# The w_gate products of six wide tiles as seven block products, in pairs with those of w_val

## The chip, the core and the metric

The kernel runs on one core of a Trainium2 chip. A core has five engines that work side by side, each through its own instructions in order: TensorE (PE in the profile; its weight loads are PEld), VectorE (DVE), ScalarE (ACT), GpSimd (POOL) and SyncE (SP). They wait for each other on semaphores. PE writes its products to PSUM, here eight banks of 128 x 512 fp32; all other data lies in SBUF. The metric is the device time of one execution in microseconds (us); lower is better. All times below are us unless another unit stands beside them.

## The reference

Sliding-window causal attention (8 batches, 8 heads, 576 positions of 64 values, window 64) is followed by a gated feed-forward layer on the 4608 rows of 512 values that it gives:

```python
scores = scale * np.matmul(q, k.transpose(0, 1, 3, 2))
mask = (rel >= 0) & (rel < 64)              # rel = pos[:, None] - pos[None, :]
attn = softmax(np.where(mask, scores, -1e9))
x = np.matmul(attn, v)                      # as 4608 x 512
gate = np.maximum(x @ w_gate, 0.0)          # 512 x 1536
val = x @ w_val                             # 512 x 1536
return (gate * val @ w_out)                 # 1536 x 512
```

## The kernel before

The 4608 rows are taken in ten tiles: tiles 0 to 3 of 384 rows (narrow), tiles 4 to 9 of 512 rows (wide). For each tile there is a hidden stage (x times w_gate and w_val, relu, product: g_sb) and an output stage (g_sb times w_out, to PSUM, by ACT to SBUF, by an SP transfer to memory). The attention of the coming tiles is woven in between: loads of q, k and v are issued on POOL's queue (L173, L199), POOL or DVE spreads v (L208, L210), DVE transposes q and k (L193), PE makes scores (L253), ACT takes exp (L287, L389), DVE masks (L292, L394), PE multiplies by v (L311, L422), DVE normalises and transposes into xt, the tile's x (channels on the partitions, four chunks of 128).

The order of all engines is written by hand. A planner, `Weaver` (W), holds a clock in us that follows PE's work and a heap of callbacks with due times; `W.at(t, fn)` plans one, `W.advance` issues those that are due before PE's next product is issued, `W.pop` issues the next one early. What is issued goes at once into its engine's queue, so due times set the order in the queues, not the times on the chip.

In the narrow tiles (`hidden`) four relus of w_gate's products go by ACT to a tile `r4` (two buffers), then w_val's four products are multiplied with them by DVE.

In the wide tiles (`fast_hidden`) w_val's product is made by a scheme of Strassen's kind (Winograd's form): a product of 2 x 2 blocks takes seven block products, P1 to P7, in place of eight. The blocks halve the channels (k), the columns of w_val (HF = 6 chunks of 128 apart) and the 512 rows of the tile (HT = 256). It needs four sums of blocks of w_val, `vs`, formed once by POOL (`w_form`, L480, planned during tile 2), and four of x per tile, `xc`, formed by DVE (`x_form`, L459). A tile's hidden stage is three groups j of 4 chunks each. One block product is four matmuls of 256 columns (L573); one w_gate product is four matmuls of 512 columns (L582), with four such in a group and a relu for each (L586). The order of a group on PE is

```python
P1, gate(2), P6, P2, gate(3), P5, P7, gate(0), P4, gate(1), P3
```

P1, P6, P7 and P4 are added up in one bank A, of which ACT takes a copy (`snap`, L593) after P1, after P6 and after P7; P2 goes to bank B, P5 and P3 to bank C. DVE adds a copy to B or C (`vsum`, L600): P1's copy with P2, P7's copy with P5 and P6's copy with P5 + P3 are three of the four quarters of val, and what stands in A after P4 is the fourth, which DVE multiplies with its relu straight from the bank (L613). The other three products relu x val are POOL's (L606). `bank()` hands out PSUM banks in the order in which they became free.

The output stage of a wide tile (`fast_output`) goes over four blocks of 128 rows (L658, 12 matmuls each); the first two need the products of the first 256 rows, the last two those of the second half. Ahead of the blocks come the next tile's products with v (two halves) and the scores of the tile after it (two quads). k and q loads are planned by `plan_batch`, 12 us of the planner's clock ahead of a given time (`qk_ahead`).

Of the kernel before, what the change touches and what calls it, by code (L numbers as in the profile page):

```python
# [15 lines left out]
SUB = mybir.AluOpType.subtract  # L16
ONE_ONE = struct.unpack("<f", struct.pack("<I", 0x3C003C00))[0]


# [27 lines left out]
def kernel(  # L47
# [10 lines left out]
    nc = tc.nc  # L58
# [34 lines left out]
    wo = persist.tile([128, NF, DM], FP16)  # L93
    HF = NF // 2
    vs = persist.tile([128, 4, 2, 128 * HF], FP16)
    qTs = [persist.tile([128, 2, S, 2], FP16, name=f"qT{i}") for i in range(2)]
    kTs = [persist.tile([128, 2, 64 + S, 2], FP16, name=f"kT{i}") for i in range(2)]

# [265 lines left out]
    def bank():  # L364

        while not free:
            W.pop()
        return free.pop(0)
# [83 lines left out]
    def x_form(t, n):  # L452

        if t not in xcs:
            xcs[t] = x_sb.tile([128, 4, 2, HT], FP16, name="xc", tag="xt")
        xt, xc = xt_tile(t), xcs[t]
        b11, b12, b21, b22 = (xt[:, 2 * k:2 * k + 2, HT * h:HT * h + HT] for k in range(2) for h in range(2))
        x, y = ((b12, b11), (b22, xc[:, 0]), (b22, b12), (b21, xc[:, 1]))[n]
        nc.vector.tensor_tensor(xc[:, n], x, y, SUB)  # L459
        if n == 3:  # L460
            normed[0] = t

    def values(t, hh, T, banks=None):

        t_pv(t, hh, banks or [bank() for _ in range(3)], banks is None)
        W.clock += 0.62
        W.at(T + 0.7, lambda: t_recip(t, hh))
        for i, k in enumerate((2, 0, 1)):
            W.at(T + 1.2 + 0.5 * i, lambda k=k: t_norm(t, hh, k))
        W.at(T + 2.7, lambda: t_turn(t, hh))  # L470
        for n in ((0,), (1, 2, 3))[hh]:
            W.at(T + 4.0 + 0.4 * n, lambda n=n: x_form(t, n))

    def w_form(n, j):

        c = slice(256 * j, 256 * j + 256)
        f = slice(256 * j + 128 * HF, 256 * j + 128 * HF + 256)
        a11, a12, a21, a22 = wv[:, 0:2, c], wv[:, 2:4, c], wv[:, 0:2, f], wv[:, 2:4, f]
        x, y, op = ((a21, a22, ADD), (vs[:, 0, :, c], a11, SUB), (a11, a21, SUB), (a12, vs[:, 1, :, c], SUB))[n]
        nc.gpsimd.tensor_tensor(vs[:, n, :, c], x, y, op)  # L480

    def plan_batch(b, load, trans):
        for i, (name, hh) in enumerate((n, hh) for n in "kq" for hh in range(2)):
# [23 lines left out]
    def hidden(t, spans, f0=0, f1=NF, each=1):  # L507
# [18 lines left out]
            done.update(dict.fromkeys(range(f, f + w), c0 + n))  # L526

        for fb in range(f0, f1, each):
            r4 = f_sb.tile([128, 4, WT], FP32, name="r4", bufs=2)
            r_sbs = {}  # L530
            for i, wt in enumerate((wg, wv)):
                for c0, f in ((c0, f) for c0, _ in spans for f in range(fb, fb + each, w)):
# [6 lines left out]
                                             xt[:, c, c0:c0 + n], start=(c == 0), stop=(c == NC - 1))  # L539
                        W.clock += 4 * (n + 7) / 2400.0  # L540
                    if i == 0:
                        r_sb = r_sbs[c0, f] = r4[:, len(r_sbs)]
                        W.at(W.clock, lambda r_sb=r_sb, h=h: relu(r_sb, h))
                    else:
                        W.at(W.clock, lambda f=f, c0=c0, r_sb=r_sbs[c0, f], h=h: gate(f, c0, r_sb, h))

    def fast_hidden(t):

        g_sb, done = gs[t] = g_sb_p.tile([128, NF, WT], FP16, name="g_sb"), {}
        xt, xc = xt_tile(t), xcs[t]  # L550
        b11, b12, b21, b22 = (xt[:, 2 * k:2 * k + 2, HT * h:HT * h + HT] for k in range(2) for h in range(2))
        halves = lambda ap: ap.rearrange("p f (h n) -> p f h n", h=2)
        pair = lambda ap: ap.rearrange("p (f n) -> p f n", f=2)

        def group(j):
            c = slice(256 * j, 256 * j + 256)
            f = slice(256 * j + 128 * HF, 256 * j + 128 * HF + 256)
            r4 = f_sb.tile([128, 4, WT], FP32, name="r4", bufs=2)
            rh = halves(r4)
            gh = halves(g_sb)  # L560
            at = {}
            forms = {"P1": (wv[:, 0:2, c], b11), "P2": (wv[:, 2:4, c], b21), "P3": (vs[:, 3, :, c], b22),
                     "P4": (wv[:, 2:4, f], xc[:, 3]), "P5": (vs[:, 0, :, c], xc[:, 0]),
                     "P6": (vs[:, 1, :, c], xc[:, 1]), "P7": (vs[:, 2, :, c], xc[:, 2])}

            def product(name, to, first):
                W.advance(W.clock)
                if first:
                    at[to] = bank()
                w, x = forms[name]  # L570
                for i in range(2):
                    for k in range(2):
                        nc.tensor.matmul(at[to][:, HT * i:HT * i + HT], w[:, k, 128 * i:128 * i + 128], x[:, k],  # L573
                                         start=(first and i == 0 and k == 0), stop=(k == 1), skip_group_check=True)
                W.clock += 4 * (HT + 7) / 2400.0

            def gate(n):
                W.advance(W.clock)
                to = bank()
                ff = 2 * j + n % 2 + HF * (n // 2)  # L580
                for k in range(NC):
                    nc.tensor.matmul(to, wg[:, k, 128 * ff:128 * ff + 128], xt[:, k], start=(k == 0), stop=(k == NC - 1))  # L582
                W.clock += 4 * (WT + 7) / 2400.0

                def relu():
                    nc.scalar.activation(r4[:, n], to, ACT.Relu)  # L586
                    free.append(to)
                W.at(W.clock, relu)

            def snap(name):  # L590
                def copy():
                    at[name] = f_sb.tile([128, 512], FP32, name="snap", bufs=5)
                    nc.scalar.copy(at[name], at["A"])  # L593
                W.at(W.clock, copy)

            def add(delay, to, name, last, n, h):

                def summed():
                    v = f_sb.tile([128, 512], FP32, name="vsum", bufs=4)
                    nc.vector.tensor_tensor(v, at[to], at[name], ADD)  # L600
                    at["summed", n, h] = True
                    if last:
                        free.append(at[to])

                    def mult():
                        nc.gpsimd.tensor_tensor(gh[:, 2 * j + HF * n:2 * j + HF * n + 2, h], rh[:, 2 * n:2 * n + 2, h], pair(v), MUL)  # L606
                        done[2 * j + HF * n, h] = done[2 * j + HF * n + 1, h] = True
                    W.at(max(W.clock, at["relus", n]) + 0.7, mult)
                W.at(W.clock + delay, summed)

            def direct():
                def mult():
                    nc.vector.tensor_tensor(gh[:, 2 * j + HF:2 * j + HF + 2, 0], rh[:, 2:4, 0], pair(at["A"]), MUL)  # L613
                    free.append(at["A"])
                    done[2 * j + HF, 0] = done[2 * j + HF + 1, 0] = True
                W.at(W.clock + 0.2, mult)

            T = W.clock
            at["relus", 1], at["relus", 0] = T + 3.7, T + 6.8
            product("P1", "A", True)  # L620
            snap("a1")
            gate(2)
            product("P6", "A", False)
            snap("u2")
            product("P2", "B", True)
            add(0.1, "B", "a1", True, 0, 0)
            gate(3)
            product("P5", "C", True)
            product("P7", "A", False)
            snap("u3")  # L630
            add(0.8, "C", "u3", False, 1, 1)
            gate(0)
            product("P4", "A", False)
            direct()
            gate(1)
            while ("summed", 1, 1) not in at:
                W.pop()
            product("P3", "C", False)
            add(0.1, "C", "u2", True, 0, 1)

        for j in range(NF // 4):
            group(j)

    F_LAST = [f for j in range(NF // 4) for f in (2 * j + HF, 2 * j + HF + 1, 2 * j, 2 * j + 1)]

# [73 lines left out]
    with tc.manual_schedule():  # L719
# [132 lines left out]
        def ahead(t):  # L852
# [94 lines left out]
```

## Time and profile before

| | |
|---|---|
| median of 3 runs | 322.11 |
| lowest, highest run | 321.64, 323.05 |
| the profiled execution: span, first to last instruction | 320.2 |
| instructions | 9481 |
| granted PE clock, mean | 0.995 |
| DMA moved | 29.52 MB, 92 GB/s mean |
| POOL multiplications relu x val (L606) | 54 of 1.276, 68.1 in all |
| sums on DVE (L600) | 54 of 0.691, 37.3 |
| relus of the wide tiles on ACT (L586) | 72 of 0.600, 43.2 |
| snaps on ACT (L593) | 54 of 0.586, 31.6 |
| transposes of q and k on DVE (L193) | 32 of 1.24, 39.6 |
| w_val's sums on POOL (L480) | 12 of 1.15 to 1.21, 14.1 |
| x's sums on DVE (L459) | 24 of 0.42 to 0.52, 11.3 |

How to read the lines that follow: an entry of the group table or the timeline names the source line, the engine, the operation, then output<-inputs, the shape and the count; a time in brackets is how long the engine was idle before it, with what it waited for. A line of stages gives, for each engine, its busy time and number of instructions in that stretch of the span. The busy time of an engine adds the spans of its instructions, of which neighbours can overlap, so a start-to-start distance can be shorter than the duration. The stages of the wide tiles in this execution: the hidden stages begin at 122.3, 157.0, 190.0, 222.9, 255.8 and 287.2 and end at 143.8, 176.7, 209.7, 242.6, 275.5 and 306.9.

### The profile page before, as it was taken

Reading aid. Unit: us, or ns where it says so; the run is one execution under the profiler, and the core shown is the slowest. Engines: PE = TensorE matmul, PEld = TensorE weight load, DVE = VectorE, ACT = ScalarE, POOL = GpSimd, SP = SyncE. Lnnn points to the kernel's source line nnn. Section 1 sums busy time; section 2 is a strip of 40 time slices with the busy share of each in tenths; the row PEclk is TensorE's granted clock in tenths of the full one; section 3 lists DMA queues with packets and bytes.
Section 4 is the critical chain, followed back from the end, with each engine's and each line's share of the span. In section 5 each row is a group of like instructions: output and inputs, shape, how many; then the busy total and the mean of one; then the engine's idle time right before and its main releaser. Section 6 shows DMA issues by size and latency. Waiting matters only on the chain.

```text
span 320.2 us, 9481 instructions
## 1 busy us (share of the span) xinstructions
PE 308.8 (96%) x4077; PEld 190.1 (59%) x4077; DVE 203.2 (63%) x397; ACT 158.1 (49%) x310; POOL 177.8 (56%) x206
## 2 busy tenths in 40 slices
PE   4799999999899999999999999999999999999996
PEld 2586958655546555665566556655665566546654
DVE  6937962667993996779576857686337734643420
ACT  3644325533524616752765276627652666326632
POOL 8859336215988506799168925980495036404540
PEclk9889999999999999999999999999999999999999
DMA  8999998946299149806910691039001100020002
GB/s 218 183 196 205 194 120 161 171 98 99 30 174 165 21 90 160 57 1 104 219 36 0 97 220 43 2 50 127 35 0 34 69 34 3 2 98 35 0 33 102
DMA packets 52491, 29.52 MB, mean 92 GB/s; under 512 B 38880, under 2 KB 43872, under 8 KB 52448
## 3 DMA queue, kind: packets, MB, share of 16 engines
q0 software_dynamic: 46688, 18.29, 49.3%
q1 hardware_dynamic: 5616, 10.55, 9.3%
q8 instruction: 32, 0.52, 0.7%
q14 instruction: 11, 0.09, 0.1%
q10 hardware_dynamic: 144, 0.07, 0.1%
HBM read 37.75 MB, written 9.44 MB: 147 GB/s over the span
## 4 chain that ended last, share of the span: by engine, by line
PE 89%; DVE 3%; ACT 2%; POOL 2%; DMA 2%; issue 1%; DVEq 0%; POOLq 0%
PE bank L658 19%; PE bank L582 19%; PE bank L538 17%; PE bank L573 17%; PE bank L673 10%; PE bank L253 3%; PE bank L422 2%; DVE p L292 2%; DMA v<-in_v_dram 2%; ACT pw L389 1%; PE bank L311 1%; DVE g_sb L525 1%; PE bank L703 1%; POOL v L199 1%; DVE qT L193 0%
## 5 line engine op out<-in xcount | busy, mean ns | idle before, releaser
L606 POOL TENSOR_TENSOR g_sb<-r,vsum 128x512 f16<-128x512 f32 x54 | 68.1, 1276 | 77.7 <-DVE vsum L600 75.7
L600 DVE TENSOR_TENSOR vsum<-bank,snap 128x512 f32<-128x512 f32 x54 | 37.3, 691 | 60.1 <-PE bank L573 36.5
L582 PE MATMUL bank<-xt,wg 128*128 128x512 f16 x288 | 73.9, 379 | 0.0
L658 PE MATMUL bank<-wo,g_sb 128*128 128x512 f16 x276 | 62.9, 380 | 0.0
L586 ACT ACTIVATE r<-bank 128x512 f32<-128x512 f32 x72 | 43.2, 600 | 32.3 <-PE bank L582 32.3
L658 PEld LDWEIGHTS <-g_sb 128*128 128x128 f16 x276 | 25.5, 98 | 28.9
L582 PEld LDWEIGHTS <-wg 128*128 128x128 f16 x288 | 28.2, 98 | 18.6
L525 DVE TENSOR_TENSOR g_sb<-r,bank 128x384 f16<-128x384 f32 x48 | 25.9, 550 | 20.3 <-PE bank L538 18.8
L522 ACT ACTIVATE r<-bank 128x384 f32<-128x384 f32 x48 | 23.7, 496 | 29.4 <-PE bank L538 20.3
L573 PEld LDWEIGHTS <-vs 128*128 128x128 f16 x288 | 28.0, 98 | 15.6 <-issue 1.6
L538 PE MATMUL bank<-xt,wg 128*128 128x192 f16 (+1 forms) x256 | 36.5, 296 | 0.5 <-DVE g_sb L525 0.4
L663 ACT COPY o_sb<-bank 128x512 f32<-128x512 f32 x23 | 13.5, 586 | 45.2 <-PE bank L658 43.2
L593 ACT COPY snap<-bank 128x512 f32<-128x512 f32 x54 | 31.6, 586 | 8.4 <-PE bank L573 8.4
L199 POOL DMA_DIRECT2D v<-in_v_dram x41 | 34.7, 865 | 1.8 <-DMA q<-in_q_dram 1.0
L538 PE MATMUL bank<-xt,wv 128*128 128x192 f16 (+1 forms) x256 | 34.3, 286 | 0.0
L673 PE MATMUL bank<-wo,g_sb 128*128 128x512 f16 x144 | 32.8, 379 | 0.2 <-DVE g_sb L525 0.2
L538 PEld LDWEIGHTS <-wg 128*128 128x128 f16 x256 | 24.3, 102 | 9.8 <-issue 0.9
L573 PE MATMUL bank<-xc,vs 128*128 128x256 f16 x216 | 29.4, 272 | 0.4 <-ACT snap L593 0.4
L208 POOL COPY v<-v 64x512 f16<-64x512 f16 (+1 forms) x22 | 16.1, 732 | 23.7 <-DMA v<-in_v_dram 22.6
L538 PEld LDWEIGHTS <-wv 128*128 128x128 f16 x256 | 22.9, 98 | 8.1
L394 DVE TENSOR_TENSOR pw<-pw,mask 128x512 f16<-128x512 f16 x48 | 20.2, 437 | 11.2 <-ACT pw L389 10.5
L389 ACT ACTIVATE pw<-bank 128x512 f16<-128x512 f32 x48 | 25.9, 608 | 1.5 <-PE bank L253 1.0
(69 smaller groups left out, 358.6 us busy)
## 6 DMA issues: line engine op xcount, KB each, us to landing
out_dram<-o_sb SPq DMA_DIRECT2D x35, 256.0 KB, 3.0
k<-in_k_dram POOLq DMA_DIRECT2D x15, 288.0 KB, 5.3
q<-in_q_dram POOLq DMA_DIRECT2D x15, 288.0 KB, 7.3
v<-in_v_dram POOLq DMA_DIRECT2D x31, 128.0 KB, 8.0
wg<-in_moe_w_gate_dram POOLq DMA_DIRECT2D x6, 256.0 KB, 6.4
wv<-in_moe_w_val_dram POOLq DMA_DIRECT2D x6, 256.0 KB, 8.2
wo<-in_moe_w_out_dram POOLq DMA_DIRECT2D x3, 512.0 KB, 11.9
v<-in_v_dram POOLq DMA_DIRECT2D x10, 64.0 KB, 5.9
```

Of the source, the lines that this page charges most:

```text
L199: nc.gpsimd.dma_start(v16s[b % 2][lo:hi, g, :, 0:64], v[b, :, 64 * g - 64 + lo:64 * g - 64 + hi].rearrange("h p d -> p h d"))
L389: nc.scalar.activation(d["p"][g].rearrange("p n c -> p (n c)"), d["st"][g], ACT.Exp, scale=scale)
L525: nc.vector.tensor_tensor(g_sb[:, f:f + w, c0:c0 + n], part(r_sb), part(h2), MUL)
L538: nc.tensor.matmul(h[:, b * n:b * n + n], wt[:, c, (f + b) * 128:(f + b) * 128 + 128], xt[:, c, c0:c0 + n], start=(c == 0), stop=(c == NC ...
L573: nc.tensor.matmul(at[to][:, HT * i:HT * i + HT], w[:, k, 128 * i:128 * i + 128], x[:, k], start=(first and i == 0 and k == 0), stop=(k == ...
L582: nc.tensor.matmul(to, wg[:, k, 128 * ff:128 * ff + 128], xt[:, k], start=(k == 0), stop=(k == NC - 1))
L586: nc.scalar.activation(r4[:, n], to, ACT.Relu)
L593: nc.scalar.copy(at[name], at["A"])
L600: nc.vector.tensor_tensor(v, at[to], at[name], ADD)
L606: nc.gpsimd.tensor_tensor(gh[:, 2 * j + HF * n:2 * j + HF * n + 2, h], rh[:, 2 * n:2 * n + 2, h], pair(v), MUL)
L658: nc.tensor.matmul(op, g_sb[:, f, 128 * sub:128 * sub + 128], wo[:, f], start=(i == 0), stop=(i == NF - 1))
L673: nc.tensor.matmul(op, g_sb[:, f, bass.ds(sub * 128, 128)], wo[:, f], start=(f == 0), stop=(f == NF - 1))
```

## The change

w_gate's products in the wide tiles are now made in the same way as w_val's. POOL forms four sums of w_gate's blocks (`us`), planned from 42.0 on the planner's clock, during tiles 0 and 1. A group is now P1 to P7 for w_gate (i = 0) and w_val (i = 1) alternately, 14 block products. Each of the two has its own bank A, B and C. Snaps and sums of the two go to the halves of one SBUF tile `pr` (six buffers, 4 KB a partition each; the narrow tiles take two of these for one `r4`). A sum is written in place over its snap. The relu of w_gate's sums is now ACT's, in place in SBUF, once for each of three quarters; of the fourth, ACT takes the relu from bank A into `r`, and DVE multiplies it with w_val's bank A. The next group's P1 is issued ahead of this group's end (in the first group before P4, in the second between P4 and P3). Three of the four sums of x per tile (n = 0, 2, 3) go from DVE to POOL. The loads of k and q for one batch are planned 6 us ahead in place of 12.

```diff
     vs = persist.tile([128, 4, 2, 128 * HF], FP16)
+    us = persist.tile([128, 4, 2, 128 * HF], FP16)
...
-        nc.vector.tensor_tensor(xc[:, n], x, y, SUB)
+        (nc.vector if n == 1 else nc.gpsimd).tensor_tensor(xc[:, n], x, y, SUB)
...
-        for n in ((0,), (1, 2, 3))[hh]:
-            W.at(T + 4.0 + 0.4 * n, lambda n=n: x_form(t, n))
-    def w_form(n, j):
+        for n, x in (((0, 4.0),), ((1, 4.0), (2, 4.1), (3, 5.0)))[hh]:
+            W.at(T + x, lambda n=n: x_form(t, n))
+    def w_form(wt, n, j):
+        to = us if wt is wg else vs
         c = slice(256 * j, 256 * j + 256)
         f = slice(256 * j + 128 * HF, 256 * j + 128 * HF + 256)
-        a11, a12, a21, a22 = wv[:, 0:2, c], wv[:, 2:4, c], wv[:, 0:2, f], wv[:, 2:4, f]
-        x, y, op = ((a21, a22, ADD), (vs[:, 0, :, c], a11, SUB), (a11, a21, SUB), (a12, vs[:, 1, :, c], SUB))[n]
-        nc.gpsimd.tensor_tensor(vs[:, n, :, c], x, y, op)
+        a11, a12, a21, a22 = wt[:, 0:2, c], wt[:, 2:4, c], wt[:, 0:2, f], wt[:, 2:4, f]
+        x, y, op = ((a21, a22, ADD), (to[:, 0, :, c], a11, SUB), (a11, a21, SUB), (a12, to[:, 1, :, c], SUB))[n]
+        nc.gpsimd.tensor_tensor(to[:, n, :, c], x, y, op)
...
-            r4 = f_sb.tile([128, 4, WT], FP32, name="r4", bufs=2)
+            r2s = [f_sb.tile([128, 2, WT], FP32, name="pr", bufs=6) for _ in range(2)]
...
-                        r_sb = r_sbs[c0, f] = r4[:, len(r_sbs)]
+                        r_sb = r_sbs[c0, f] = r2s[len(r_sbs) // 2][:, len(r_sbs) % 2]
...
+        kinds = ((wg, us), (wv, vs))
+        at = {}
+        def operands(name, wt, sums, j):
+            c = slice(256 * j, 256 * j + 256)
+            f = slice(256 * j + 128 * HF, 256 * j + 128 * HF + 256)
+            return {"P1": (wt[:, 0:2, c], b11), "P2": (wt[:, 2:4, c], b21), "P3": (sums[:, 3, :, c], b22),
+                    "P4": (wt[:, 2:4, f], xc[:, 3]), "P5": (sums[:, 0, :, c], xc[:, 0]),
+                    "P6": (sums[:, 1, :, c], xc[:, 1]), "P7": (sums[:, 2, :, c], xc[:, 2])}[name]
+        TO = {"P1": "A", "P6": "A", "P7": "A", "P4": "A", "P2": "B", "P5": "C", "P3": "C"}
+        AFTER = {"P6": ("P1", "snap"), "P7": ("P6", "snap"), "P4": ("P7", "snap"), "P3": ("P7", "sum")}
+        def product(j, name, i):
+            W.advance(W.clock)
+            if name in AFTER:
+                before, what = AFTER[name]
+                while (j, what, before, i) not in at:
+                    W.pop()
+            first = name in ("P1", "P2", "P5")
+            if first:
+                at[j, TO[name], i] = bank()
+            to = at[j, TO[name], i]
+            w, x = operands(name, *kinds[i], j)
+            for m in range(2):
+                for k in range(2):
+                    nc.tensor.matmul(to[:, HT * m:HT * m + HT], w[:, k, 128 * m:128 * m + 128], x[:, k],
+                                     start=(first and m == 0 and k == 0), stop=(k == 1), skip_group_check=True)
+            W.clock += 4 * (HT + 7) / 2400.0
+            at[j, "ran", name, i] = True
+        def snap(j, name, i):
+            if i == 0:
+                at[j, "pair", name] = f_sb.tile([128, 2, WT], FP32, name="pr", bufs=6)
+            pr = at[j, "pair", name]
+            def copy():
+                nc.scalar.copy(pr[:, i], at[j, "A", i])
+                at[j, "snap", name, i] = True
+            W.at(W.clock, copy)
+        def add(j, name, bank_name, i, n, h, delay):
+            def summed():
+                while (j, "snap", name, i) not in at:
+                    W.pop()
+                pr, to = at[j, "pair", name], at[j, bank_name, i]
+                nc.vector.tensor_tensor(pr[:, i], to, pr[:, i], ADD)
+                at[j, "sum", name, i] = True
+                if name != "P7":
+                    free.append(to)
+                if i == 0:
+                    def relu():
+                        nc.scalar.activation(pr[:, 0], pr[:, 0], ACT.Relu)
+                    W.at(W.clock + 1.1, relu)
+                else:
+                    def mult():
+                        f = 2 * j + HF * n
+                        nc.gpsimd.tensor_tensor(gh[:, f:f + 2, h], pair(pr[:, 0]), pair(pr[:, 1]), MUL)
+                        done[f, h] = done[f + 1, h] = True
+                    W.at(W.clock + 1.2, mult)
+            W.at(W.clock + delay, summed)
+        def direct(j, i):
+            if i == 0:
+                def relu():
+                    at[j, "r"] = f_sb.tile([128, WT], FP32, name="r", bufs=2)
+                    nc.scalar.activation(at[j, "r"], at[j, "A", 0], ACT.Relu)
+                    free.append(at[j, "A", 0])
+                    at[j, "relu"] = True
+                W.at(W.clock, relu)
+            else:
+                def mult():
+                    while (j, "relu") not in at:
+                        W.pop()
+                    f = 2 * j + HF
+                    nc.vector.tensor_tensor(gh[:, f:f + 2, 0], pair(at[j, "r"]), pair(at[j, "A", 1]), MUL)
+                    free.append(at[j, "A", 1])
+                    done[f, 0] = done[f + 1, 0] = True
+                W.at(W.clock + 0.2, mult)
+        def step(j, name):
+            for i in range(2):
+                product(j, name, i)
+                if name in ("P1", "P6", "P7"):
+                    snap(j, name, i)
+                if name == "P2":
+                    add(j, "P1", "B", i, 0, 0, 0.1)
+                if name in ("P5", "P7") and (j, "ran", "P5", i) in at and (j, "ran", "P7", i) in at:
+                    add(j, "P7", "C", i, 1, 1, 0.1 if name == "P5" else 0.8)
+                if name == "P4":
+                    direct(j, i)
+                if name == "P3":
+                    add(j, "P6", "C", i, 0, 1, 0.1)
+        last = NF // 4 - 1
+        step(0, "P1")
+        for j in range(last + 1):
+            for name in ("P2", "P6", "P5", "P7") if j == 0 else ("P6", "P2", "P7", "P5"):
+                step(j, name)
+            tail = [(j, "P4"), (j + 1, "P1"), (j, "P3")] if j else [(j + 1, "P1"), (j, "P4"), (j, "P3")]
+            for jj, name in tail:
+                if jj <= last:
+                    step(jj, name)
...
-        def qk_ahead(t, T, gaps):
+        def qk_ahead(t, T, gaps, lead=12.0):
...
-                plan_batch(b, T - 12.0, [T + x for x in gaps])
+                plan_batch(b, T - lead, [T + x for x in gaps])
...
-                        W.at(T + 12.0 + 6.4 * j + 1.6 * n, lambda at=at, j=j: w_form(at, j))
+                        W.at(T + 12.0 + 6.4 * j + 1.6 * n, lambda at=at, j=j: w_form(wv, at, j))
...
-                qk_ahead(NS + 2, T + 27.6, SLOTS)
+                qk_ahead(NS + 2, T + 27.6, SLOTS, 6.0)
...
+        for j in range(NF // 4):
+            for n, at in enumerate((0, 1, 3, 2)):
+                W.at(42.0 + 8.8 * j + 2.2 * n, lambda at=at, j=j: w_form(wg, at, j))
```

More of the change, by code (lines that the diff above doesn't have):

```diff
@@ L16 @@
 SUB = mybir.AluOpType.subtract
+MAX = mybir.AluOpType.max
 ONE_ONE = struct.unpack("<f", struct.pack("<I", 0x3C003C00))[0]
@@ L550, in fast_hidden @@
         xt, xc = xt_tile(t), xcs[t]
-        b11, b12, b21, b22 = (xt[:, 2 * k:2 * k + 2, HT * h:HT * h + HT] for k in range(2) for h in range(2))
-        halves = lambda ap: ap.rearrange("p f (h n) -> p f h n", h=2)
+        b11, b21, b22 = xt[:, 0:2, 0:HT], xt[:, 2:4, 0:HT], xt[:, 2:4, HT:WT]
+        gh = g_sb.rearrange("p f (h n) -> p f h n", h=2)
         pair = lambda ap: ap.rearrange("p (f n) -> p f n", f=2)
-        def group(j):
+        kinds = ((wg, us), (wv, vs))
+        at = {}
+        def operands(name, wt, sums, j):
@@ L556, in group @@
             c = slice(256 * j, 256 * j + 256)
             f = slice(256 * j + 128 * HF, 256 * j + 128 * HF + 256)
[L558 to L583, printed above, removed]
+            return {"P1": (wt[:, 0:2, c], b11), "P2": (wt[:, 2:4, c], b21), "P3": (sums[:, 3, :, c], b22),
+                    "P4": (wt[:, 2:4, f], xc[:, 3]), "P5": (sums[:, 0, :, c], xc[:, 0]),
+                    "P6": (sums[:, 1, :, c], xc[:, 1]), "P7": (sums[:, 2, :, c], xc[:, 2])}[name]
@@ L585, in relu @@
+        def direct(j, i):
+            if i == 0:
                 def relu():
-                    nc.scalar.activation(r4[:, n], to, ACT.Relu)
-                    free.append(to)
+                    at[j, "r"] = f_sb.tile([128, WT], FP32, name="r", bufs=2)
+                    nc.scalar.activation(at[j, "r"], at[j, "A", 0], ACT.Relu)
+                    free.append(at[j, "A", 0])
+                    at[j, "relu"] = True
                 W.at(W.clock, relu)
[L590 to L609, printed above, removed]
@@ L611, in direct @@
-            def direct():
-                def mult():
-                    nc.vector.tensor_tensor(gh[:, 2 * j + HF:2 * j + HF + 2, 0], rh[:, 2:4, 0], pair(at["A"]), MUL)
-                    free.append(at["A"])
-                    done[2 * j + HF, 0] = done[2 * j + HF + 1, 0] = True
-                W.at(W.clock + 0.2, mult)
[L618 to L638, printed above, removed]
@@ L639, in group @@
-            add(0.1, "C", "u2", True, 0, 1)
-        for j in range(NF // 4):
-            group(j)
+            else:
+                def mult():
+                    while (j, "relu") not in at:
[4 more added lines that the diff above has]
+                    done[f, 0] = done[f + 1, 0] = True
+                W.at(W.clock + 0.2, mult)
```

## The prediction

> **What bounds the kernel now.** The page first: engine shares and the chain of waits.
>
> ```profile
> PE 308.8 (96%) x4077; PEld 190.1 (59%) x4077; DVE 203.2 (63%) x397; ACT 158.1 (49%) x310; POOL 177.8 (56%) x206
> PE 89%; DVE 3%; ACT 2%; POOL 2%; DMA 2%; issue 1%; DVEq 0%; POOLq 0%
> ```
>
> TensorE (PE) is the bound nearly everywhere, so PE work that is removed is worth its full time until another engine makes PE wait. So I ask how full the others are, stage by stage (busy time of each engine in a hidden stage: tiles 4, 5 and 7, and the output stage between 6 and 7).
>
> ```profile
> core 0: us, PE busy (x) PEld busy (x) DVE busy (x) ACT busy (x) POOL busy (x), PEclk, DMA share, GB/s
> 122.30:143.80 21.50, 20.72 (x203) 13.35 (x204) 14.99 (x25) 16.01 (x30) 17.48 (x19) 1.00 0.63 67
> 157.00:176.70 19.70, 19.70 (x135) 12.81 (x134) 12.05 (x16) 12.34 (x22) 13.05 (x13) 1.00 0.39 48
> 209.70:222.90 13.20, 13.20 (x305) 6.83 (x305) 10.72 (x27) 6.17 (x12) 6.92 (x8) 1.00 0.87 107
> 222.90:242.60 19.70, 19.70 (x133) 12.79 (x131) 7.43 (x12) 12.31 (x22) 13.01 (x13) 1.00 0.04 14
> ```
>
> PE has no gap in tiles 5 to 9; tile 4 has some. Tiles 4 to 6 carry extra VectorE (DVE) work: each has four q/k transposes in its hidden stage (L193). The clock is 1.00 throughout. Next the chain inside tile 7, for the price of PE's pieces:
>
> ```profile
> 223.52 0.86 PE bank L582 x4
> 224.38 0.94 PE bank L573 x8
> 225.32 0.86 PE bank L582 x4
> 226.19 0.87 PE bank L573 x8
> ```
>
> A w_gate group of four 512-wide matmuls costs 0.864, one block product (four 256-wide) 0.435. Then the time from start to start on ACT and DVE, from the timeline:
>
> ```profile
> 223.16 0.59 ACT L663 COPY o_sb<-bank 128x512 f32<-128x512 f32 x1 [0.66 <-ACT pw L389]
> 223.65 0.59 ACT L593 COPY snap<-bank 128x512 f32<-128x512 f32 x1
> 227.78 0.69 DVE L600 TENSOR_TENSOR vsum<-bank,snap 128x512 f32<-128x512 f32 x1 [1.63 <-ACT snap L593]
> 228.40 0.69 DVE L613 TENSOR_TENSOR g_sb<-r,bank 128x512 f16<-128x512 f32 x1
> 142.56 1.25 DVE L193 STREAM_TRANSPOSE qT<-q 128x576 f32<-128x576 f32 x1
> 143.65 0.68 DVE L613 TENSOR_TENSOR g_sb<-r,bank 128x512 f16<-128x512 f32 x1
> ```
>
> Instructions overlap: an ACT copy lasts 0.59 but the next starts 0.49 later; a sum lasts 0.69 with pitch 0.61; a transpose 1.25 with pitch 1.08. From the same timelines: four masks (L394) take 1.89, pitch 0.34; ACT starts about 0.67 after the start of the product it reads, DVE about 0.74 after, DVE 0.09 after an ACT end, PE 0.05 after either.
>
> **PE.** Each of 18 groups (three per tile) loses 4 x 0.864 and 7 x 0.435 = 6.50 and gets 14 x 0.435 = 6.09: 0.41 to 0.43 each, 1.3 a tile, 7.8 in all if nothing waits. The new weights `us` are read as `vs` is: same 256-wide rows.
>
> **The other engines in one group.** ACT had 4 relus and 3 snaps; it gets 6 snaps, one relu from PSUM and 3 relus of sums in SBUF: 10 x 0.49 = 4.9 of 6.09. A relu from SBUF has no row; bounds: 0.50 (L522, 384 wide) and 0.67 (the SBUF cast L186, 576 wide), no overlap; I take pitch 0.49, since L586 lasts 0.60 like the copies. Even 4 x 0.67 + 6 x 0.49 = 5.6 fits. The Trainium skill (Perfetto Trace Analysis, Optimizing Scalar/DVE Operations) gives ScalarE some 40 ns more per instruction from SBUF than from PSUM; by it the ten would take 5.0, with the same result. DVE had 3 sums and one product, it gets 6 and one: 7 x 0.61 = 4.3. POOL keeps 3 multiplications (L606).
>
> **Do products wait for snaps?** Bank A is re-entered four slots later (P6g, P6v, P2g, P2v, then P7g; g is w_gate, v w_val): 4 x 0.435 = 1.74. Needed: 0.67 + 0.59 + 0.05 = 1.31, and 1.37 for v, which queues behind g. Margin 0.37 to 0.43: no wait in a tile where ACT and DVE have room. P3 must wait for the sum of P7 from the same bank: in the second group P5g has slot 22, its sum starts 22 x 0.435 + 0.74 = 10.31 and ends 11.0; P3g's slot is 28 x 0.435 = 12.18. So tiles 7, 8, 9: -1.3 each, **-3.9**.
>
> **Tiles 5 and 6.** The new DVE order puts a transpose between the sums. From the tile's start: ACT reads the first group's P4g after snaps of the next P1 (5.11, 5.60), at 6.09 to 6.69; DVE's direct product starts 6.78, the sums of P6 at 7.39 and 8.00. Second group: sum P1g 8.61, transpose 9.22, sum P1v 10.30, sum P7g 10.91, transpose 11.52, sum P7v 12.60 to 13.29. P3v had its slot at 12.62 and starts at 13.34: 0.72 lost. Third group: P1g 15.38, P1v 15.99, transpose 16.60, P7g 17.68 to 18.37, P7v to 18.98; P3g's slot 18.12 becomes 18.42, P3v's 18.86 becomes 19.03: 0.48 lost. 1.2 of 1.3 is given back: **-0.1 each**.
>
> **Tile 4** carries eight exps, eight masks and four transposes beside its groups, and PE waits there already:
>
> ```profile
> 124.08 0.60 PE L573 MATMUL bank<-xc,vs 128*128 128x256 f16 x4 [0.35 <-ACT snap L593]
> 126.54 0.66 PE L253 MATMUL bank<-qT,kT 32*128 32x64 f16 x61 [0.43 <-ACT pw L389]
> ```
>
> After: ACT starts at 122.47 with o_sb, exp, snap P1g, exp, snap P1v, each 0.49 apart; P1v's snap ends 125.02, so P6v starts 125.07 instead of 124.45. The scores come behind two more exps, to 126.65. P5g is at 126.65, P7g at 127.52. ACT then alternates: relu 126.88, exp, snap P7g 128.20, exp, snap P7v, exp, snap P1g, exp, snap P1v, and the relu that the direct product needs at 131.63, to 132.23. DVE does that product at 132.32 and has no gap from there: 13 steps of 0.61 and 3 transposes of 1.08 later, at 143.49, the sum of the last P7v starts, ends 144.18, and P3v ends its slot at 144.67. Before, the stage ended at 143.83: **+0.8**. So no gain where DVE's 21 x 0.61 + 8 x 0.34 + 4 x 1.08 = 19.9 is over PE's 18.9.
>
> **x_form on POOL.** Three of four go from DVE (0.42 to 0.52) to POOL, 1.15 to 1.21 by the f16 rows of L480: 3.6 a tile. They sit in the output stage, behind the last multiplications and four k/q issues (0.55 each), ahead of five v issues (0.87). Tile 5: last multiplication at 23.5, issues to 25.7, three forms to 30.1; the next tile starts at 32.7 and needs the last form 12 slots later. But POOL's f16 work holds up DVE's masks:
>
> ```profile
> 80.68 2.50 POOL L480 TENSOR_TENSOR vs<-wv 128x512 f16<-128x512 f16 x2
> 80.24 4.38 DVE L292 TENSOR_TENSOR p<-p,mask 128x384 f16<-128x384 f16 x4 [1.04 <-ACT p L287]
> ```
>
> Four masks took 4.38 there against 1.51 free of it (59.66). The three forms can block DVE for 3.6 at most: 10.7 - 1.3 + 3.6 = 13.0 in a stage of 13.2, and the first sum is due 1.6 into the tile. I take 0; without that room it costs what DVE is late. The Trainium skill (Perfetto Trace Analysis, Optimizing Scalar/DVE Operations) warns that moving work between these two may not help, as they share an SBUF port; by it the move saves DVE nothing and the sum stays as it is, since DVE's output stage has the room.
>
> **Twelve forms of w_gate on POOL**, 12 x 1.2 = 14.4, from 35.8, where POOL idles 9.7 and later 8.8. Five run to 41.9 in the first gap; the first mask at 41.10 is up to 0.8 late, 44.47 needs it: covered. The k/q issues at 48.4 go to 52 and the v issues at 50.5 to 57.8; landing (5.3, 7.3, 8.0) gives 62 and 68.5, needed at 66.7 and 86. Masks at 56.7 and 60 are 1 late, with 0 to 0.3 of it at the product at 62.4: **+0.2**, between 0 and 1. If the cover fails (k after 66.7), DVE holds the gates of tile 2.
>
> **The moved k/q loads** (lead 6 for 12): batch 5 is issued at 122.3 to 124.5 and lands by 132, its first transpose is at 133.5. In tiles 5 and 6 they follow all nine multiplications; landing by 154 for 160.7. **Pairs in place of r4** (six buffers): PE waited 0.4 in all for gates (L538), so at most -0.4; I take 0. Banks: C takes what the earlier A freed two steps before: 0. SP's 35 output issues stay.
>
> **Sum:** 3 x -1.3, 2 x -0.1, +0.8, +0.2 = -3.1. The profiled execution, 320.2, becomes 317.1. The median of the runs is 1.9 above that span: 322.1 becomes **319.0**.
>
> **Rivals.** (a) The whole gain: DVE's transposes find gaps, and tile 4 waits no more than now: -7.8, 314.3. For it: 12 of 19.7 is DVE's load in tile 5 now. Against: the order in DVE's queue. (b) No gain: every re-entry into bank A waits. If the snap's round trip is 0.43 longer than 1.37, PE waits 0.06 three times a group, 18 x 0.18 = 3.2, which eats the 3.1: 322.2. For it: ACT now waits in order for DVE's sums between the snaps, three relus a group. Against: these sums end 0.4 to 1.0 before ACT comes to them in tile 8. (c) Slower: the port decides. If the masks of an output stage each wait for POOL (8 x 1.1 instead of 8 x 0.34), DVE enters the next tile 3 to 6 late rather than up to 1.6; what is over 2.2 (1.6 and 0.6 of margin) stalls P3 in five tiles. At 4 late: 5 x 1.8 = 9, 328; it passes no change at 2.8 late. For it: the row at 80.24; against: POOL has only three forms to block with.
>
> **Chances.** Forecast 0.48, (a) 0.18, (b) 0.18, (c) 0.16. Half a per cent, 1.6, is what a measurement here can tell from no change: faster (below 320.5) 0.66, same 0.17, slower 0.17. The unknown costs (tile 4 by 1.5, tiles 5 and 6 by 0.8 each, a relu's pitch) put the likeliest case at 316 to 321; reaching into (a) and (b): 315.0 to 322.8.
>
> **What would show it.** Tiles 7 to 9: hidden stages of 18.3 to 18.5, products without waits. Tiles 5, 6: 19.4 to 19.6, PE waiting for DVE ahead of P3. Tile 4: about 22.4, ACT waits early, DVE waits late. ACT 17 and DVE 14 to 19 busy per stage. Wrong if PE waits for snaps in tile 8, for POOL at an output's first rows, or if masks run into the next tile.

## The result, and the profile after

| | before | after |
|---|---|---|
| median of 4 runs each, same chip | 321.88 | 318.12 |
| lowest, highest run | 321.50, 323.05 | 317.93, 318.92 |
| ratio to before, 95% interval | | 0.9885 (0.9861 to 0.9908) |
| span of the profiled execution | 320.2 | 317.2 |

The change makes the kernel 1.2% faster: 3.8 by the medians, 3.0 by the two profiled spans. The forecast was 319.0, with a span of 317.1. The profiled execution after is the longest of its four (318.92); the other three have spans of 316.2 to 316.4. Why is seen at its start, in PE's timeline (start, duration, engine, line, operation, in brackets the idle time before it and its releaser):

```profile
15.15 4.03 PE L541 MATMUL bank<-xt,wg 128*128 128x192 f16 x30 [0.91 <-DMA wg<-in_moe_w_gate_dram]
```

The first narrow tile waited 0.91 for the load of w_gate, which the change doesn't touch. The profile of before has no such wait. From there to tile 4 these two executions run at a constant distance, and tile 4 begins at 122.90 against 122.27. (In e9, the same kernel once more, this wait is 0.32, and tile 4 begins at 122.08.) So 0.63 of this profile is a late start, and the change itself is worth 3.6 here, close to the 3.8 of the medians.

The page of after, busy time of the engines, then the chain of waits by engine:

```profile
PE 303.1 (96%) x4293; PEld 210.9 (66%) x4293; DVE 237.2 (75%) x433; ACT 181.7 (57%) x364; POOL 212.9 (67%) x236
PE 80%; DVE 8%; ACT 4%; DMA 2%; POOL 2%; issue 2%; DVEq 0%; ACTq 0%; POOLq 0%
```

PE's busy time falls by 5.7, DVE's rises by 34, POOL's by 35, ACT's by 24. On the chain PE goes from 89% to 80%, and DVE from 3% to 8%: part of what PE gave up is now waited for on DVE. The groups behind it (busy time and mean ns, then idle time before them):

```profile
L604 DVE TENSOR_TENSOR pr<-bank,pr 128x512 f32<-128x512 f32 x108 | 68.9, 682 | 24.6 <-PE bank L583 17.2
L594 ACT COPY pr<-bank 128x512 f32<-128x512 f32 x108 | 58.0, 594 | 12.4 <-PE bank L583 8.7
L610 ACT ACTIVATE pr<-pr 128x512 f32<-128x512 f32 x54 | 34.7, 642 | 8.0 <-DVE pr L604 7.8
```

By stages (tiles 4, 5 and 7, and the output stage between 6 and 7; the same columns as before):

```profile
122.90:145.20 22.30, 20.59 (x237) 16.86 (x239) 19.25 (x31) 19.86 (x38) 17.41 (x21) 1.00 0.77 93
158.40:178.00 19.60, 19.09 (x192) 16.48 (x194) 16.33 (x25) 15.84 (x30) 14.78 (x16) 1.00 0.58 64
210.70:224.00 13.30, 13.30 (x303) 6.89 (x288) 11.92 (x25) 6.58 (x13) 9.98 (x11) 1.00 0.30 69
224.00:242.30 18.30, 18.30 (x191) 16.23 (x193) 12.25 (x20) 15.77 (x30) 12.55 (x13) 1.00 0.46 42
```

In tile 7 PE is busy throughout; in tiles 4 and 5 it isn't, with DVE at 19.25 of 22.3 and 16.33 of 19.6. From start of hidden stage to start of the work behind it, in the timelines:

| hidden stage of tile | 4 | 5 | 6 | 7 | 8 | 9 | sum |
|---|---|---|---|---|---|---|---|
| before | 21.49 | 19.70 | 19.70 | 19.70 | 19.70 | 19.61 | 119.9 |
| after | 22.27 | 19.42 | 19.43 | 18.43 | 18.44 | 18.34 | 116.3 |
| difference | +0.78 | -0.28 | -0.27 | -1.27 | -1.26 | -1.27 | -3.6 |
| forecast | +0.8 | -0.1 | -0.1 | -1.3 | -1.3 | -1.3 | -3.3 |

The output stages keep their length (13.21 before and 13.22 after between tiles 6 and 7). A hidden stage whose engines keep up takes 18.43; tile 5 takes 0.99 more. PE's timeline of tile 5, third column the engine:

```profile
170.63 0.60 PE L583 MATMUL bank<-xt,us 128*128 128x256 f16 x4
171.67 0.60 PE L583 MATMUL bank<-xt,vs 128*128 128x256 f16 x4 [0.43 <-DVE pr L604]
```

and DVE's of the same time:

```profile
167.58 1.25 DVE L195 STREAM_TRANSPOSE kT<-k 128x576 f32<-128x576 f32 x1
168.67 1.27 DVE L604 TENSOR_TENSOR pr<-bank,pr 128x512 f32<-128x512 f32 x2
169.87 1.23 DVE L195 STREAM_TRANSPOSE qT<-q 128x576 f32<-128x576 f32 x1
170.94 0.68 DVE L604 TENSOR_TENSOR pr<-bank,pr 128x512 f32<-128x512 f32 x1
```

The sum at 170.94 is that of the second group's P7 of w_val. P3 of w_val, which adds into the same bank, had its slot 0.435 after 170.63 and began 1.04 after it: 0.60 lost. The transpose at 169.87 stands in DVE's queue ahead of that sum, and nothing in this group needs it.

### The profile page after: what moved, and what is told of

Its sections match the earlier page's. It is cut to its first block, busy times and chain, and to the rows that moved or that the text cites. A ratio compares the mean times of both kernels' runs of the same rounds, so it can differ in the third digit from the quotient of the medians.

```text
span 317.2 us, 10104 instructions
## 1 busy us (share of the span) xinstructions
PE 303.1 (96%) x4293; PEld 210.9 (66%) x4293; DVE 237.2 (75%) x433; ACT 181.7 (57%) x364; POOL 212.9 (67%) x236
## 4 chain that ended last, share of the span: by engine, by line
PE 80%; DVE 8%; ACT 4%; DMA 2%; POOL 2%; issue 2%; DVEq 0%; ACTq 0%; POOLq 0%
PE bank L583 27%; PE bank L676 19%; PE bank L541 17%; PE bank L691 10%; DVE pr L604 3%; PE bank L255 3%; PE bank L424 2%; DMA wg<-in_moe_w_gate_dram 2%; DVE p L294 2%; ACT pr L594 2%; ACT pw L391 2%; POOL v L201 1%; DVE g_sb L528 1%; PE bank L721 1%; PE bank L313 1%
## 5 line engine op out<-in xcount | busy, mean ns | idle before, releaser
L615 POOL TENSOR_TENSOR g_sb<-pr 128x512 f16<-128x512 f32 x54 | 68.1, 1277 | 45.0 <-ACT pr L610 42.6
L604 DVE TENSOR_TENSOR pr<-bank,pr 128x512 f32<-128x512 f32 x108 | 68.9, 682 | 24.6 <-PE bank L583 17.2
L594 ACT COPY pr<-bank 128x512 f32<-128x512 f32 x108 | 58.0, 594 | 12.4 <-PE bank L583 8.7
L528 DVE TENSOR_TENSOR g_sb<-pr,bank 128x384 f16<-128x384 f32 x48 | 25.8, 548 | 20.8 <-PE bank L541 19.4
L525 ACT ACTIVATE pr<-bank 128x384 f32<-128x384 f32 x48 | 23.6, 495 | 29.9 <-PE bank L541 20.7
L610 ACT ACTIVATE pr<-pr 128x512 f32<-128x512 f32 x54 | 34.7, 642 | 8.0 <-DVE pr L604 7.8
L583 PE MATMUL bank<-xc,us 128*128 128x256 f16 x216 | 32.4, 273 | 0.0
L583 PEld LDWEIGHTS <-us 128*128 128x128 f16 x288 | 28.1, 98 | 5.1 <-issue 1.6
L541 PEld LDWEIGHTS <-wg 128*128 128x128 f16 x256 | 23.9, 101 | 10.7 <-DMA wg<-in_moe_w_gate_dram 1.4
L391 ACT ACTIVATE pw<-bank 128x512 f16<-128x512 f32 x48 | 26.0, 612 | 1.2 <-PE bank L255 0.8
L461 POOL TENSOR_TENSOR xc<-xt 128x512 f16<-128x512 f16 x12 | 13.9, 1166 | 19.0 <-DVE xt L449 19.0
```

The source lines that it names most:

```text
L391: nc.scalar.activation(d["p"][g].rearrange("p n c -> p (n c)"), d["st"][g], ACT.Exp, scale=scale)
L528: nc.vector.tensor_tensor(g_sb[:, f:f + w, c0:c0 + n], part(r_sb), part(h2), MUL)
L541: nc.tensor.matmul(h[:, b * n:b * n + n], wt[:, c, (f + b) * 128:(f + b) * 128 + 128], xt[:, c, c0:c0 + n], start=(c == 0), stop=(c == NC ...
L583: nc.tensor.matmul(to[:, HT * m:HT * m + HT], w[:, k, 128 * m:128 * m + 128], x[:, k], start=(first and m == 0 and k == 0), stop=(k == 1), ...
L594: nc.scalar.copy(pr[:, i], at[j, "A", i])
L604: nc.vector.tensor_tensor(pr[:, i], to, pr[:, i], ADD)
```

## The experiments

The runs were made on three chips, each beside its own runs of before: e1 to e4 with a median of 322.61 (9 runs), e5 to e8 with 321.85 (9) and e9 to e11 with 321.91 (11). A ratio is to before on the same chip.

**e1: no transposes beside the wide tiles.**

```diff
+        if b >= 5:
+            return
```

This stands in front of the transposes of q and k (L195), so those of batches 5 to 7 are left out, and later attention reads older q and k.

> The changed kernel without DVE's transposes of q and k for batches 5 to 7, which stood in the hidden stages of tiles 4, 5 and 6 (12 of 1.25; the attention of the later rows is then made from old q and k). Theory (the transposes between DVE's sums are what P3 waits for): tiles 5 and 6 fall from 19.3 to 18.3 like tile 7, tile 4 from 22.2 to some 21.3 (its waits for ACT stay, those for DVE ahead of the last P3 go): 2.9 less than the changed kernel's 318.1, about 315.2. Rival (the waits come from ACT's order, or from POOL holding the port): tiles 5 and 6 keep at least half of their 1.0, 317 or more.

315.52, ratio 0.9784 (0.9764 to 0.9805). Tiles 5 and 6 take 18.43 each, tile 4 21.18. So the 0.99 that tiles 5 and 6 lack of the full gain comes from the transposes alone, and so does 1.1 of tile 4. The rest of tile 4 stays.

**e2: the transposes stay, but at other places in DVE's queue, tiles 5 and 6.** The planned times of the four transposes in a hidden stage are moved. One goes to the tile's start, one stays behind the first group's sums of P1, one goes between the second group's sums of P1 and those of P7, and one behind its sums of P6; none splits a pair of sums any more.

```diff
+        LATER = (-1.2, 2.6, 8.28, 12.68)
-                    qk_ahead(t + 3, T + WIDE_T, SLOTS)
+                    qk_ahead(t + 3, T + WIDE_T, LATER)
```

> The changed kernel with the same twelve transposes, but in tiles 5 and 6 placed where DVE is idle: one at the tile's start, one after the first P1 sums as now, one between the second P1 sums and P7 sums, one after the second P6 sums. Theory (it is the order in DVE's queue, not DVE's load): no wait ahead of P3, tiles 5 and 6 at 18.3, 2.0 less: 316.1. Rival (DVE's load: 21 x 0.61 and 4 x 1.08 are 17.1 of 18.3, any order makes waits): 0.5 less at most, 317.6 or more.

316.32, ratio 0.9814 (0.9798 to 0.9831). Tiles 5 and 6 take 18.43 each with all the work done; tile 4 is as in after (22.27). PE's waits from tile 4 to tile 6 are now those of tile 4 alone. What was lost in tiles 5 and 6 was order, not DVE's capacity.

**e3: tile 4 as well.**

```diff
-                qk_ahead(NS + 2, T + 27.6, SLOTS, 6.0)
+                qk_ahead(NS + 2, T + 27.6, (2.6, 6.53 + 0.8, 17.6, 17.7), 6.0)
```

> As the retimed kernel of tiles 5 and 6, and in tile 4 the two q transposes go behind the last sums of its hidden stage (one had stood ahead of the last P1 sums). Theory: the last P7 sums start 1.1 earlier, the waits of 0.62 and 0.16 ahead of the last P3 go, 0.8 less than the other retimed kernel: 315.3. If tile 4 is held by ACT alone, nothing more is gained: 316.1.

315.70, ratio 0.979 (0.9775 to 0.9806). Tile 4 takes 21.33. PE's waits in tiles 4 to 6 (engine, line, what it waited for, then total, times, longest):

```profile
PE bank L583 <- ACT pr L594: 0.4, 1, 0.4
PE bank L583 <- ACT pw L391: 0.3, 1, 0.3
PE bank L676 <- POOL g_sb L615: 0.3, 1, 0.3
PE bank L255 <- ACT pw L391: 0.3, 1, 0.3
```

Three of the four are for ACT, which has the eight exps (L391) of the next tile between its snaps. The waits for DVE ahead of the last P3 are gone. The list shows no wait for DVE, yet P3 of the first group still starts late. DVE's, POOL's and PE's timelines of tile 4:

```profile
129.13 0.97 DVE L396 TENSOR_TENSOR pw<-pw,mask 128x512 f16<-128x512 f16 x1 [0.84 <-ACT pw L391]
130.03 1.28 DVE L604 TENSOR_TENSOR pr<-bank,pr 128x512 f32<-128x512 f32 x2
...
128.52 1.29 POOL L615 TENSOR_TENSOR g_sb<-pr 128x512 f16<-128x512 f32 x1
...
130.76 0.60 PE L583 MATMUL bank<-xt,us 128*128 128x256 f16 x4
131.36 0.60 PE L583 MATMUL bank<-xt,vs 128*128 128x256 f16 x4
```

A mask takes 0.97 beside a multiplication of POOL's, where its neighbours take 0.42, and the two sums of P7 stand behind it. P3 of w_gate is 0.30 and P3 of w_val another 0.16 behind its slot. In the profile of after the same place costs 0.31 and 0.16, behind a mask of 1.92.

**e4: all four sums of x back on DVE.**

```diff
-        (nc.vector if n == 1 else nc.gpsimd).tensor_tensor(xc[:, n], x, y, SUB)
+        nc.vector.tensor_tensor(xc[:, n], x, y, SUB)
```

> The changed kernel with all four sums of x per tile on DVE again. My step took 0 for their move to POOL. Theory: DVE's output stage has the room either way, within 0.5 of 318.1. Rival (the shared port makes the move harmful, masks late): 1 to 3 less, 315 to 317. Second rival (DVE has no room for them, so that their move is needed): 1 or more above, 319 or more.

318.67, ratio 0.9891 (0.9874 to 0.9908), beside 0.9885 (0.9861 to 0.9908) of after. The move is worth nothing that can be measured here, where the two intervals overlap nearly whole. DVE's timelines say why: the first sum of tile 5 comes after an idle time of 1.54 in after,

```profile
154.57 3.87 DVE L396 TENSOR_TENSOR pw<-pw,mask 128x512 f16<-128x512 f16 x8
159.99 0.69 DVE L604 TENSOR_TENSOR pr<-bank,pr 128x512 f32<-128x512 f32 x1 [1.54 <-PE bank L583]
```

and after the same idle time in e4:

```profile
156.83 1.90 DVE L396 TENSOR_TENSOR pw<-pw,mask 128x512 f16<-128x512 f16 x4 [0.81 <-ACT pw L391]
160.26 1.29 DVE L604 TENSOR_TENSOR pr<-bank,pr 128x512 f32<-128x512 f32 x2 [1.54 <-PE bank L583]
```

The last masks end with ACT's exps, whoever makes the sums of x.

**e5: the next group's P1 no longer ahead.** Every group runs in one fixed order, still in pairs.

```diff
-            for name in ("P2", "P6", "P5", "P7") if j == 0 else ("P6", "P2", "P7", "P5"):
+            for name in ("P1", "P2", "P6", "P5", "P7", "P4", "P3"):
...
-            tail = [(j, "P4"), (j + 1, "P1"), (j, "P3")] if j else [(j + 1, "P1"), (j, "P4"), (j, "P3")]
```

> The changed kernel with each group in the order P1, P2, P6, P5, P7, P4, P3, w_gate and w_val alternating as before, but the next group's P1 no longer ahead of this group's end. P4 then follows P7 by two slots (0.87) in place of four, where the snap's round trip needs 1.31: 0.44 of wait in each group, and 0.05 to 0.1 more ahead of P3: 18 x 0.5 = 9, some of it in place of the waits of tiles 4 to 6: 325 to 327. Rival (the round trip is not what decides, PE finds other work): within 1 of 318.1.

326.14, ratio 1.0125 (1.0107 to 1.0143). P4 now follows P7 after two slots in place of four. From PE's timeline of tile 7 (rows of P7 of w_gate, P7 of w_val, P4 of w_gate):

```profile
229.88 0.60 PE L583 MATMUL bank<-xc,us 128*128 128x256 f16 x4
230.32 0.60 PE L583 MATMUL bank<-xc,vs 128*128 128x256 f16 x4
231.22 0.61 PE L583 MATMUL bank<-xc,wg 128*128 128x256 f16 x4 [0.29 <-ACT pr L594]
```

From the start of P7 to that of P4 are 1.34: this is the round trip by way of ACT's snap, put at 1.31 in the prediction. The two slots cover 0.87 of it, so 0.47 is lost in each group, and P4 of w_val loses 0.05 more. Tile 7 takes 19.95 against 18.43.

**e6: no pairs.** In each group seven products of w_gate, then seven of w_val. The next group's P1 isn't ahead either, as in e5, where that alone cost about 8.

```diff
-            for i in range(2):
+            for i in only:
...
+            for i in range(2):
+                for name in ("P1", "P2", "P6", "P5", "P7", "P4", "P3"):
+                    step(j, name, (i,))
```

> The changed kernel with the seven products of w_gate first and then the seven of w_val in each group, no look-ahead. Bank A is re-entered after two slots twice (0.44 of wait each), after one slot once (0.87), and P3 waits for its sum (0.35): 2.1 for each seven products, 36 sevens: 76 more, 385 to 400. Rival (PE's products alone decide): 318 to 327.

424.27, ratio 1.3162 (1.3118 to 1.3206), above the 385 to 400 that was expected. Three lines of its profile: PE's waits, and the granted clock in the 40 slices of the span (tenths of full speed, 9 is 90% or more):

```profile
PE bank L583 <- ACT pr L594: 43.8, 99, 1.4
PE bank L583 <- DVE pr L604: 26.4, 18, 1.8
PEclk9899999999998898999999988999899989898989
```

Re-entry into a bank now waits 99 times for a snap and 18 times, once in each group, for a sum. That is 70 of the 106 over after. PE's busy time also rises, from 303.1 to 339.8, for the same 4293 matmuls, and the mean granted clock is 0.952 against 0.995. How much of the 37 is the clock, and how much are the modelled ends of matmuls in front of a wait, was not taken apart.

**e7: in tile 4, the exps out of ACT's way.** e3, and the third quad of scores in the output stage before tile 4 is made 2.6 earlier.

```diff
-                for qd, x in ((0, 6.0), (1, 9.2), (2, 22.6), (3, 25.8)):
+                for qd, x in ((0, 6.0), (1, 9.2), (2, 20.0), (3, 25.8)):
```

> The retimed kernel of tiles 4, 5 and 6 with the third quad of scores planned 2.6 earlier in tile 3's output stage, so that its four exps run on ACT before tile 4 begins, where ACT is idle. Theory (tile 4's early waits, 0.38, 0.26 and 0.30, come from snaps and scores queued behind exps on ACT): 0.6 to 0.9 less than the retimed kernel's 315.7: 314.8 to 315.1. Rival (the scores then wait for DVE's norms and hold up the output stage): 315.7 or more.

315.17, ratio 0.9793 (0.9777 to 0.9808). Tile 4 begins where it did in e3 (122.10 and 122.08) and takes 20.25, 1.08 less; the waits of 0.4 for a snap and of 0.3 ahead of the scores are gone. By the ratio, though, it is no better than e3 (0.979), so the gain of one profiled tile isn't shown in the times; e10 and e11 compare the two on one chip.

**e8: w_gate's twelve forms made twice**, to see what covers them.

```diff
-                W.at(42.0 + 8.8 * j + 2.2 * n, lambda at=at, j=j: w_form(wg, at, j))
+                W.at(42.0 + 8.8 * j + 2.2 * n, lambda at=at, j=j: (w_form(wg, at, j), w_form(wg, at, j)) and None)
```

> The changed kernel with each of w_gate's twelve sums formed twice on POOL, 14.4 more work in its queue in tiles 0 to 2. My step took 0.2 for the twelve. Theory (POOL's idle time covers them, with room left): 0 to 1 more, 318.1 to 319.1. Rival (the cover was just used up; the k loads of batch 2 land after DVE asks for them, and the gates of tile 2 wait): 2 to 5 more, 320 to 323.

325.22, ratio 1.011 (1.0091 to 1.013): 7 more than after, above the 2 to 5 of the rival, and by another way. No load of k is late. What happened is in the timeline of DVE, POOL and PE at 42 to 48:

```profile
42.86 3.31 DVE L294 TENSOR_TENSOR p<-p,mask 128x384 f16<-128x384 f16 x3
43.45 5.01 POOL L483 TENSOR_TENSOR us<-wg 128x512 f16<-128x512 f16 x4
...
46.20 1.26 DVE L210 COPY v<-v 64x1024 f16<-64x1024 f16 x1
...
47.51 0.31 PE L313 MATMUL bank<-v,p 128*32 128x65 f16 x16 [2.60 <-DVE v L210]
```

In after, the same three masks and the same copy of v met a POOL without forms:

```profile
42.98 0.88 DVE L294 TENSOR_TENSOR p<-p,mask 128x384 f16<-128x384 f16 x3
43.90 0.42 DVE L210 COPY v<-v 64x1024 f16<-64x1024 f16 x1
```

Beside POOL's forms each mask takes 1.1 in place of 0.3 and the copy 1.26 in place of 0.42, and PE waits 2.60 for v and then 0.85 for the next part of it. Behind these waits PE's granted clock, the third number from the end, is 0.50 for a while:

```profile
49.00:52.00 3.00, 3.00 (x30) 1.17 (x19) 2.36 (x6) 0.00 (x0) 2.76 (x5) 0.50 0.00 0
```

The 21 output products that start at 49.23 take about 1.4 longer than before. From 62.31 to 69.3 the next masks are held up in the same way, and PE loses 1.3 more at the products with v that need them. With the 3.9 lost at 44 to 49 these make 6.6 up to tile 4; tile 4 itself takes 22.65, 0.4 more. So what covers the forms isn't idle time on POOL, of which there is more, but time in which DVE has no such work.

**e9 to e11: after, e3 and e7 once more**, together on one chip.

> The changed kernel itself, on one chip beside the two versions below: 318.1, ratio 0.988 to 0.989, so that they can be compared without the difference between chips.

> The version with the transposes of tiles 4, 5 and 6 retimed: 2.9 less than the changed kernel on the same chip, ratio 0.979.

> The retimed version with the third quad of scores earlier. Its profile showed tile 4 at 20.25 where the retimed one has 21.33, but the two were timed on different chips. Theory (the 1.08 is on the path): 1.0 less than the retimed version on the same chip, ratio 0.976. Rival (given back elsewhere): no difference.

| | median | ratio to before |
|---|---|---|
| e9, the change as it is | 318.16 | 0.9883 (0.9859 to 0.9906) |
| e10, the edits of e3 | 316.04 | 0.9815 (0.979 to 0.984) |
| e11, the edits of e7 | 315.59 | 0.9791 (0.9767 to 0.9816) |

Both versions beat the change by 2.1 and 2.6, and before by about 6. Between the two, 0.45 in place of the 1.0 expected, with intervals that overlap. The profiled execution of e11 is the longest of its five (316.0), and shows one thing that costs it. In DVE's, POOL's and PE's timelines of tile 4:

```profile
128.88 1.77 DVE L396 TENSOR_TENSOR pw<-pw,mask 128x512 f16<-128x512 f16 x1 [0.98 <-ACT pw L391]
...
129.01 1.35 POOL L615 TENSOR_TENSOR g_sb<-pr 128x512 f16<-128x512 f32 x1
...
131.30 0.60 PE L583 MATMUL bank<-xt,us 128*128 128x256 f16 x4 [0.93 <-DVE pr L604]
```

The same mask at 128.07 in e7's profile took 0.43, though POOL's multiplication began 0.10 after it there, too, and no product waited for DVE. Tile 4 takes 20.86 in this execution, 20.25 in that of e7. How often a mask is held in e7's order, two profiles can't tell.

## Why the prediction was right, point by point

- **Price of the products.** 14 x 0.435 in place of 4 x 0.864 + 7 x 0.435: hidden stages of 18.43, 18.44 and 18.34 in tiles 7 to 9, inside the 18.3 to 18.5 that was named, without a wait. -1.3 each was exact.
- **Re-entry into bank A.** Four slots of 1.74 against a round trip of 1.31: e5 shows the trip to be 1.34, and two slots to be too few. The margin of about 0.4 was real; rival (b), which needed a trip 0.43 longer, falls.
- **Tiles 5 and 6.** The place and the cause were right: P3 waits for sums of P7, behind transposes. The forecast losses were 0.72 and 0.48; measured were 0.60 in the second group and 0.40 (0.24 + 0.16) in the third. The sums have a pitch of 0.60 and not 0.61, and transposes 1.07 to 1.09; seven steps in a row add such differences up. -0.3 each in place of -0.1. e1 and e2 show that the order was the cause.
- **Tile 4.** +0.8, as forecast. DVE's queue ended last, as forecast: the sums of the last P7 held the last P3. e1 and e3 put about 1.0 on its transposes, and the profile of e7 1.08 on ACT's exps in front of the snaps. The prediction had P6 of w_val 0.62 late behind the exps (measured 0.65), and yet took the end from DVE's queue alone, so that the share of each stayed open; ACT's part without DVE's was not tried. What it left out is the mask that takes 1.92 beside POOL's first multiplication and puts the first group's P3 about 0.5 late.
- **The relu from SBUF.** It lasts 0.642, and from one such relu to the next instruction are 0.53, where relus from PSUM have 0.49 (ACT in tile 5: 169.52, 170.01, 170.54). The prediction took 0.49 for both. The Trainium skill (Perfetto Trace Analysis, Optimizing Scalar/DVE Operations) has some 40 ns between the two spaces, and this trace agrees: 0.04. It cost nothing, since ACT has 15.8 of 18.4 in tile 7.
- **Twelve forms of w_gate.** The term of +0.2 was about right, and at the place that was named, the product with v at 62. In before (first two rows) and in e9:

```profile
59.66 1.51 DVE L292 TENSOR_TENSOR p<-p,mask 128x384 f16<-128x384 f16 x4 [0.56 <-ACT p L287]
61.93 1.03 PE L311 MATMUL bank<-v,p 128*32 128x65 f16 x96
59.55 2.64 DVE L294 TENSOR_TENSOR p<-p,mask 128x384 f16<-128x384 f16 x4
61.58 1.20 PE L313 MATMUL bank<-v,p 128*32 128x65 f16 x96
```

  The four masks are held up by the forms, and the product takes 0.17 longer: up to it e9 runs 0.35 earlier than before, and from there on 0.18; e7 and e10 lose about as much there. In the profile of after, with its late start, nothing is lost there. The cover that was named, POOL's gaps, wasn't the right one (e8).
- **x_form, k/q loads, pairs, banks.** 0 each, and no wait in after points to one of them; of the four only x_form was tried by itself (e4).
- **Rival (c), the port.** The mechanism is there (e8: DVE's masks at three times their duration; in tile 4 a held mask costs the changed kernel about 0.5) but not where the rival had it, at the three forms of x: the 8 masks ahead of tile 5 took 3.87, and DVE was still 1.54 early. Of **rival (a)**, the whole gain, tiles 7 to 9 have theirs; e2 and e3 show that tiles 5 and 6 could have had it, too, by planned times alone.

Together: the terms of the hidden stages came to -3.3 and measured -3.6, a difference that lies in tiles 5 and 6; the forms of w_gate came to +0.2 and measured 0 in after and 0.17 in e9. That the profiled span (317.2) meets the forecast one (317.1) so closely is luck, owed to the late start of 0.63 in that execution. The medians, 318.12 against 319.0, are the fairer comparison, and 0.2 of their distance comes from before, whose median is 322.11 in the forecast's three runs and 321.88 in the four of the result.

## What to carry to other kernels

An engine's queue is in order, so when an edit gives an engine new work that the bound engine waits for, move the unrelated work in that queue behind it: here other planned times brought 2.1 on top of the change's 3.8, without an instruction more or less. Two independent accumulations that alternate hide the read-out of each other's banks, and the slots between two uses of a bank can be counted against the measured round trip before anything is built. Idle time on POOL isn't enough to cover work given to it: in e8 it was covered only where DVE had no masks or copies at the same time.

## What the runs showed of the hardware that was not expected

- POOL's f16 sums held up not only DVE's masks (1.1 for 0.3) but also its copies of v, which have one input (1.26 for 0.42), when they ran back to back (e8). The Trainium skill (SBUF — State Buffer, Who interferes with whom) has both: operations with two inputs in SBUF contend with POOL's reads, and copies can contend in a faster mode. DVE's sums, which read one input from PSUM, stayed at 0.67 to 0.69 throughout; that, too, is as the page has it for one input in SBUF.
- Which of the two is held when a mask and a multiplication of POOL begin within 0.13 of each other differed between two profiles of the same kernel: 0.43 and 1.77 for the mask (e7 and e11). In the order of after, the corresponding mask of tile 4 took 1.92 to 1.94 in the profiles of after, e1, e2, e9 and e10, and 0.42 in those of e3 and e4, where a later one took 0.97 and 0.57.
- With PE waiting in every group (e6), the granted clock fell to 0.952 in the mean, below 0.9 in 11 of the 40 slices. That it was the waiting that brought it down was not tried; e8 has the like once: 0.50 from 49 to 52, after PE had been busy for only 0.64 of the 4.0 before.
